# Shared rows copied one pair earlier in GpSimd's order, a small copy ahead of each early gather, and the first zeros made first

## The chip, the cores and the metric

The kernel runs on one core of a Trainium2 chip. The metric is the device time of one execution in microseconds (us), the median of the runs that are given. One execution is also recorded by the hardware profiler; its records give the span from the first to the last instruction and every engine's instructions in it.

## The reference, cut to what matters

```python
# attention: 8 batches, 8 heads, 576 positions, 64 wide; window 32, dilation 4
rel = pos[:, None] - pos[None, :]
mask_plain = (rel >= 0) & (rel < window)                                       # heads 0-3
mask_dil = (rel >= 0) & (rel < window * dilation) & (rel % dilation == 0)      # heads 4-7
scores = np.where(masks, q @ k.T / 8, -1e9)
attn = softmax(scores); x = attn @ v          # heads side by side: (8, 576, 512)
# mixture of 8 experts, one per token
logits = x @ w_gate; local_gate = sigmoid(x @ w_local)
for b, s:                                     # in order along s
    fresh_e = argmax(logits[b, s])
    e = fresh_e if s == 0 or local_gate[b, s] < 0.5 else prev_e
    prev_e = e
    out[b, s] = softmax(logits[b, s])[e] * (relu(x[b, s] @ w1[e]) @ w2[e])
```

Routing depends on the attention's result, and a token may inherit the expert of the token before it.

## The kernel before, in words

**Attention.** The host puts the positions of the dilated heads in order of their residue modulo 4, so that both kinds of head become a window of 32 neighbours. Work goes by pairs of heads: 8 batches times 4 pairs give `NPB = 32` pairs. A sequence is cut into 9 blocks of 64 queries; a block needs the 64 keys of its own block and the 32 before them, 96 in all. In SBUF the values of a pair lie in a tile `vt` of 96 partitions: rows 32 to 95 of block i are loaded from memory, and rows 0 to 31 are the last 32 rows of block i-1. These shared rows are not loaded a second time: `share(n)` (line 268) has GpSimd copy them from partitions 64 to 95 to partitions 0 to 31, for blocks 1 to 8. Block 0 has zeros there, set once. There are four such tiles (`AHEAD = 4`), used in turn.

**The loop** at line 1093 runs over n = 0 to 33. In turn n it issues the scores of pair n (TensorE, then ScalarE's exponentials with a VectorE clamp for the second half), `share(n)`, a slot for routing work (`gap`), `values(n - 1)` (line 367: products of the probabilities with `vt`, then VectorE's reciprocal into `rec` and a multiplication into `x`, once for slots 0 and 1, once for 2 to 4), on every second turn `turn` (line 390: transposes of x), another slot, the loads for pair n + 3, and the store of x. Then, if the list `rows` is not empty, one entry of it is run.

**The early gathers.** Routing of the first four batches ends in the midst of the loop (`early_tokens`, line 1082). It fills `rows` with eight indirect gathers (`rows_of`, line 842; DMA_INDIRECT of line 849) that fetch the tokens of the first two units of expert work out of the stored x. One is issued at the end of each turn from n = 26 on. The first four serve unit 0, whose `features(0)` (line 856, transposes of line 864) comes at the start of turn 33; the other four serve unit 1.

**What sets the order.** `manual_schedule` (line 216) keeps TensorE, VectorE, GpSimd and SyncE in the order in which the program text issues their instructions; each engine runs its own in that order and waits on semaphores. So GpSimd's order around the gathers is: share(26), gather 1, share(27), gather 2, share(28), gather 3, and so on to share(31), gather 6, gather 7, gather 8. Loads run on SyncE's queue; the gathers are DMAs of GpSimd's queue. PSUM tiles of the loop come from four banks (`banks`, tag "bank") used by values, turn and routing alike, and two double banks for the scores.

**After the loop** come 8 experts' worth of units of tokens (pairs of 128 tokens with seven products in place of eight, and smaller ones), with the weights streamed in.

**The start.** VectorE sets `ones` (line 203), `zero` (251), `warm` (281), then `before` (300); TensorE multiplies `warm` with itself three times (line 283), before the first scores.

The lines about which the change turns:

```python
    def share(n):
        vt = vts[n % AHEAD]
        nc.gpsimd.tensor_copy(vt[:WIN, :, 1:], vt[QB:, :, :NB - 1])
...
        if n < NPB:
            share(n)
        gap(SHARE)
        if 1 <= n <= NPB:
            values(n - 1)
...
        if rows:
            rows.pop(0)()
```

Of the kernel before, what the change touches and what calls it, by code (L numbers as in the profile page):

```python
# [10 lines left out]
F32 = mybir.dt.float32  # L11
# [11 lines left out]
P = 128  # L23
# [14 lines left out]
NPB = B * NP  # L38
UNITS = ((0, 5), (5, 9))
SLOTS = (NB + 1) // 2  # L40
# [141 lines left out]
@with_exitstack  # L182
def dilated_attn_locality_moe_kernel(
    ctx: ExitStack,
    tc: tile.TileContext,
    qk: bass.AP,
    v: bass.AP,
    wgl: bass.AP,
    w1: bass.AP,
    w2: bass.AP,  # L190
    con: bass.AP,
    adm: bass.AP,
    msk: bass.AP,
    qmk: bass.AP,
    out: bass.AP,
):
    nc = tc.nc
    keep = ctx.enter_context(tc.tile_pool(name="keep", bufs=1))
    cst = keep.tile([P, C_ALL], F32, name="cst")
    wg = keep.tile([P, DK, LW], F32, name="wg")  # L200
    ones = keep.tile([P, P], F32, name="ones")
    bad = keep.tile([1, 1], I32, name="bad")
    nc.vector.memset(ones, 1.0)

    args = (qk, v, wgl, w1, w2, con, adm, msk, qmk, out, cst, wg, ones)
    again = whole(tc, False, bad, *args)

    with tc.If(again > 0):  # L208
        whole(tc, True, bad, *args)


@with_exitstack
def whole(ctx, tc, exact, bad, qk, v, wgl, w1, w2, con, adm, msk, qmk, out, cst, wg, ones):
    nc = tc.nc
    name = "exact" if exact else "plain"
    ctx.enter_context(tc.manual_schedule(engines={ET.PE, ET.DVE, ET.Pool, ET.SP}))
# [2 lines left out]
    def pool(name, bufs, **kw):  # L219
        return ctx.enter_context(tc.tile_pool(name=name, bufs=bufs, **kw))  # L220
# [5 lines left out]
    once = pool("once", 1)  # L226
# [4 lines left out]
    def room(to, i, name, shape):  # L231
# [9 lines left out]
    ins, work, xp, xtp = (attention.enter_context(tc.tile_pool(name=name, bufs=bufs))  # L241
                     for name, bufs in (("ins", AHEAD), ("work", 2), ("xp", 3), ("xtp", 2)))
# [3 lines left out]
    def bank(shape, name):  # L246
        return banks.tile(shape, F32, name=name, tag="bank")

    rec = once.tile([P, NPB, SLOTS, 2], F32, name="rec")
    zero = work.tile([1, D // 2], F32, name="zero", bufs=1)  # L250
    nc.vector.memset(zero, 0.0)
    for to in xd:
# [11 lines left out]
    def load_values(n):  # L264
        vt = vts[n % AHEAD]
        nc.sync.dma_start(out=vt[WIN:].rearrange("p u i e -> p (u i e)"), in_=v[n])

    def share(n):
        vt = vts[n % AHEAD]
        nc.gpsimd.tensor_copy(vt[:WIN, :, 1:], vt[QB:, :, :NB - 1])  # L270

    def load(n):
        load_keys(n)
        load_values(n)

    if not exact:
        am = work.tile([P, adm.shape[1]], BF16, name="am", bufs=1)
        nc.sync.dma_start(out=am, in_=adm)
        mk = work.tile([KW, 2, S - UNITS[1][0] * QB], BF16, name="mk", bufs=1)
        warm = work.tile([P, 512], F32, name="warm", bufs=1)  # L280
        nc.vector.memset(warm, 0.0)
        for _ in range(WARM):
            nc.tensor.matmul(bank([P, 512], "cold"), lhsT=warm[:, :P], rhs=warm, start=True, stop=True)
    load_keys(0)
# [17 lines left out]
    def load_first(i, part):  # L302

        rows = FK // 4
        nc.sync.dma_start(out=raw1[i][:, part * rows:(part + 1) * rows].rearrange("p m k f -> p (m k f)"),
                          in_=w1[i, :, part * rows * D:(part + 1) * rows * D])
# [60 lines left out]
    def values(n):  # L367

        vt = loaded[n][2]
        if n % 2 == 0:  # L370
            xs[n // 2] = xp.tile([P, SLOTS, 2, 2, DH], F32, name="x")
        x = xs[n // 2]
        pr = prob.pop(n)
        for a, z in HALVES:
            pv = bank([P, z - a, 2, VW], "pv")
            for k in range(a, z):
                for u in range(2):
                    for h in range(2):
                        i = min(2 * k + h, NB - 1)
                        c, p = next((c, p) for c, p in reversed(pr) if c <= i)  # L380
                        nc.tensor.matmul(pv[h * QB:(h + 1) * QB, k - a, u], lhsT=p[:, u, (i - c) * QB:(i - c + 1) * QB],  # L381
                                         rhs=vt[:, u, i], start=True, stop=True, tile_position=(0, h * QB),
                                         skip_group_check=True)
            r = rec[:, n, a:z]
            nc.vector.reciprocal(r, pv[:, :, :, DH])
            nc.vector.tensor_tensor(x[:, a:z, n % 2], pv[:, :, :, :DH],
                                    r.unsqueeze(3).to_broadcast([P, z - a, 2, DH]), op=Alu.mult)
        del loaded[n]

    def turn(m):  # L390

        x = xs[m]
        b, g = divmod(m, 2)
        if m % (2 * GB) == 0:
            routes[b // GB] = dict(xt=xtp.tile([P, 2, CH, GS], F32, name="xt"))
        xt = routes[b // GB]["xt"]
        s = b % GB * S
        full = S // P * P
        for c in range(CH):
            tp = bank([P, S // P, P], "tp")  # L400
            for k in range(S // P):
                nc.tensor.transpose(tp[:, k], x[:, k, c].rearrange("p u d -> p (u d)"), ident)
            nc.scalar.copy(xt[:, g, c, s:s + full], tp.rearrange("p k t -> p (k t)"))
        tp = bank([P, CH, S - full], "tp")
        for c in range(CH):
            nc.tensor.transpose(tp[:, c], x[:S - full, S // P, c].rearrange("p u d -> p (u d)"),
                                ident[:S - full, :S - full])
        nc.scalar.copy(xt[:, g, :, s + full:s + S], tp)

    def store(m):  # L410

        x = xs.pop(m)
        b, g = divmod(m, 2)
        full = S // P * P
        to = xd[g][b * S:(b + 1) * S]
        nc.sync.dma_start(out=to[:full].rearrange("(k p) f -> p k f", p=P),
                          in_=x[:, :S // P].rearrange("p k g u d -> p k (g u d)"))
        nc.sync.dma_start(out=to[full:], in_=x[:S - full, S // P].rearrange("p g u d -> p (g u d)"))
# [362 lines left out]
    def gap(add=None):  # L781
        if add is not None:
            credit[0] = min(credit[0] + add, add)
        alone = False
        while waiting and not alone and (add is None or credit[0] >= 0):
            f, cost, _ = waiting.pop(0)
            credit[0] -= cost
            if f:
                f()
            alone = add is None or not waiting or waiting[0][2]  # L790
# [7 lines left out]
    def now(push):  # L798
        for f in push:
            f()  # L800
# [55 lines left out]
    def features(u):  # L856
        kind = units[u]["kind"]
        rows = rows_in(u)
        xe[u] = mw.tile([P, DK, 2 * P], F32, name="xe")
        for j in range(tiles_of(u)):  # L860
            x = xg.pop((u, j)).rearrange("p g f -> p (g f)")
            tp = bank([P, DK, P], "tp")
            for kk in range(DK):
                nc.tensor.transpose(tp[:, kk, :rows], x[:rows, kk * P:(kk + 1) * P], ident[:rows, :rows])
            nc.scalar.copy(xe[u][:, :, j * P:j * P + rows], tp[:, :, :rows])
        if kind == "pair":
            xc[u] = mw.tile([P, 4, DK // 2, P], F32, name="xc", bufs=1)
            return sums_right(xc[u], *(xe[u][:, 2 * k:2 * k + 2, j * P:(j + 1) * P]
                                       for k in range(2) for j in range(2)))
        return []  # L870
# [222 lines left out]
    for n in range(NPB + 2):  # L1093
        if n < NPB:
            (scores_exact if exact else scores)(n)
        if n < NPB:
            share(n)
        gap(SHARE)
        if 1 <= n <= NPB:
            values(n - 1)  # L1100
        if n == NPB + 1:
            assert len(rows) <= 4
            now(features(0))
        if n >= 3 and n % 2 == 1:
            turn((n - 3) // 2)
            if (n - 3) // 2 % (2 * GB) == 2 * GB - 1:
                route((n - 3) // 2 // (2 * GB), n == NPB + 1)
        gap(SHARE)
        if n + 3 < NPB:
            load(n + 3)  # L1110
        if n >= 3 and n % 2 == 1:
            store((n - 3) // 2)
        if n in (11, 14, 17, 20):
            load_first(0, (n - 11) // 3)
        if n == NPB + 1:
            weights(0, True)
            weights(1, False)
        if rows:
            rows.pop(0)()
    now(rows)  # L1120
    attention.close()
# [159 lines left out]
```

## Time and profile before

| | |
|---|---|
| runs | 667.06, 668.27, 689.95 us; median 668.27 |
| the profiled execution | 670.79 us, of which its span is 668.9 |
| granted TensorE clock | 0.997 |
| PE (TensorE) | busy 649.8 us |
| PEld (its weight loads) | busy 571.0 us |
| DVE (VectorE) | busy 373.1 us |
| ACT (ScalarE) | busy 188.7 us |
| POOL (GpSimd) | busy 185.3 us; the 32 copies of line 270 are 34.7 of it |

A row of the timeline has the start and the duration in us, the engine, the line, the operation, the tiles (out<-in), the shape and a count; in square brackets stand the idle time of the engine before it and what is taken to have ended it. Where several semaphores are waited for, the bracket names the one that came last by this record, which can be a mere coincidence. A row of the waits has who waited, for whom, the us in total, how many times, and the longest. The end of a matmul is modelled, since matmuls overlap; its start is recorded.

### The profile page before, as it was taken

The page shows a single profiled execution, that of the slowest core. Times are in us where ns is not written, and L with a number is a line of the kernel's source. Part 1 is how long each engine was busy: PE and PEld are TensorE (multiplying, and loading weights), DVE is VectorE, ACT ScalarE, POOL GpSimd, SP SyncE. Part 2 cuts the span into 40 slices and gives each one's busy share as a digit, 9 for nine tenths or more (in the row PEclk, how much of TensorE's full clock was granted, in tenths as well). Part 3 has the DMA queues.
Part 4 walks back from the last instruction along what each step waited for, and adds up shares of the span by engine and source line. Part 5 has one row for each costly group of instructions (what it writes and reads, how often), then busy time and mean ns, then how long its engine had stood idle before and what let it go on. Part 6 is the DMA issues. An engine that isn't in the chain of part 4 may idle for free. (4 is left out here: it accounts for less than half of the span.)

```text
span 668.9 us, 15284 instructions
## 1 busy us (share of the span) xinstructions
PE 649.8 (97%) x6466; PEld 571.0 (85%) x6466; DVE 373.1 (56%) x755; ACT 188.7 (28%) x348; POOL 185.3 (28%) x162
## 2 busy tenths in 40 slices
PE   8999999989999999999999999999999999999996
PEld 6989888877678999999599988997889988899893
DVE  3558578574496596373447381827373627446441
ACT  3544343432212332222223223222222232213210
POOL 3322212141024320221551252314044213041011
PEclk9999999999999999999999999999999999999998
DMA  8989889838205299474543456541054452354001
GB/s 322 306 299 318 288 264 321 250 117 318 119 33 189 64 416 368 176 274 174 198 163 130 161 187 223 238 159 50 3 189 176 184 206 99 133 212 146 1 33 49
DMA packets 29358, 126.38 MB, mean 189 GB/s; under 512 B 4222, under 2 KB 13790, under 8 KB 25313
## 3 DMA queue, kind: packets, MB, share of 16 engines
q1 hardware_dynamic: 22480, 106.10, 44.0%
q0 software_dynamic: 6800, 19.21, 8.3%
q8 instruction: 53, 0.87, 0.5%
q14 instruction: 25, 0.20, 0.1%
HBM read 142.07 MB, written 19.20 MB: 241 GB/s over the span
## 5 line engine op out<-in xcount | busy, mean ns | idle before, releaser
L973 POOL DMA_INDIRECT out_dram<-y,tok x36 | 55.0, 1528 | 297.3 <-DVE y L1042 124.3
L945 PE MATMUL hp<-xc,sum 128*128 128x128 f32 x720 | 85.7, 275 | 1.0 <-DVE sum L812 1.0
L945 PEld LDWEIGHTS hp<-xc,sum 128*128 128x128 f32 x720 | 82.9, 192 | 1.4 <-PE hp L945 1.1
L1027 PE MATMUL yp<-sum,hc 128*128 128x256 f32 x360 | 82.6, 379 | 0.0
L955 DVE TENSOR_TENSOR h<-hp,h 128x512 f32<-128x512 f32 x45 | 30.9, 689 | 90.5 <-PE hp L945 89.8
L1027 PEld LDWEIGHTS yp<-sum,hc 128*128 128x128 f32 x360 | 68.2, 190 | 9.5 <-ACT y L1035 0.2
L1042 DVE SCALAR_TENSOR_TENSOR y<-yp,gate,y 128x256 f32<-128x256 f32 x45 | 21.7, 482 | 75.0 <-issue 49.2
L270 POOL COPY vt<-vt 32x1040 f32<-32x1040 f32 x32 | 34.7, 1087 | 92.3 <-DMA vt<-in_v_dram 62.3
L945 PE MATMUL hp<-xe,raw 128*128 128x128 f32 x480 | 58.8, 276 | 0.0
L945 PEld LDWEIGHTS hp<-xe,raw 128*128 128x128 f32 x480 | 56.6, 192 | 1.8 <-issue 1.5
L1027 PE MATMUL yp<-raw,h 128*128 128x256 f32 x240 | 57.0, 380 | 0.0
L849 POOL DMA_INDIRECT xg<-xd,tok x40 | 45.7, 1142 | 38.6 <-PE hp L945 15.3
L329 PE MATMUL two<-kq 64*96 64x64 f32 x1152 | 54.7, 245 | 0.0
L329 PEld LDWEIGHTS two<-kq 64*96 64x96 f32 x1152 | 52.6, 162 | 0.0
L1027 PEld LDWEIGHTS yp<-raw,h 128*128 128x128 f32 x240 | 44.4, 190 | 5.5
L949 ACT COPY h<-hp 128x512 f32<-128x512 f32 x45 | 26.3, 585 | 79.0 <-PE hp L945 74.2
L381 PE MATMUL pv<-vt,pr 96*64 96x65 f32 x1280 | 45.9, 224 | 2.3 <-POOL vt L270 2.1
L956 ACT ACTIVATE h<-h 128x512 f32<-128x512 f32 x45 | 28.3, 630 | 67.2 <-DVE h L955 63.2
L334 DVE SCALAR_TENSOR_TENSOR pr<-two,mk 96x512 f32<-96x512 f32 x32 | 21.9, 684 | 44.7 <-ACT pr L336 28.6
L849 POOL DMA_INDIRECT xg<-xd,pos x40 | 43.0, 1075 | 12.1 <-issue 10.1
L381 PEld LDWEIGHTS pv<-vt,pr 96*64 96x64 f32 x1280 | 40.8, 137 | 5.3 <-POOL vt L270 2.6
L1035 ACT ACTIVATE y<-yp,gate 128x256 f32<-128x256 f32 x45 | 21.2, 473 | 55.7 <-PE yp L1027 49.9
(222 smaller groups left out, 1006.7 us busy)
## 6 DMA issues: line engine op xcount, KB each, us to landing
raw<-in_w_dram SPq DMA_DIRECT2D x48, 2048.0 KB
kq<-in_qk_dram SPq DMA_DIRECT2D x32, 592.0 KB
vt<-in_v_dram SPq DMA_DIRECT2D x32, 292.5 KB
xd<-x SPq DMA_DIRECT2D x16, 512.0 KB
raw<-in_w_dram SPq DMA_DIRECT2D x4, 512.0 KB
xd<-x SPq DMA_DIRECT2D x16, 64.0 KB
xg<-xd,tok POOLq DMA_INDIRECT x40
xg<-xd,pos POOLq DMA_INDIRECT x40
```

Source lines behind the costliest of these rows:

```text
L270: nc.gpsimd.tensor_copy(vt[:WIN, :, 1:], vt[QB:, :, :NB - 1])
L329: nc.tensor.matmul(sc[:KW, u, (i - a) * QB:(i - a + 1) * QB], lhsT=kt[h, i * QB:i * QB + KW], rhs=qt[h, i * QB:(i + 1) * QB], start=bool(a ...
L334: nc.vector.scalar_tensor_tensor(pr, sc[:KW, :, :w], -CEIL, mk[:, kind].unsqueeze(1).to_broadcast([KW, 2, w]), Alu.max, Alu.min)
L381: nc.tensor.matmul(pv[h * QB:(h + 1) * QB, k - a, u], lhsT=p[:, u, (i - c) * QB:(i - c + 1) * QB], rhs=vt[:, u, i], start=True, stop=True, ...
L849: nc.gpsimd.indirect_dma_start(out=x[:rows, g], out_offset=None, in_=xd[g] if units[u]["late"] else xd[g][:EARLY * GS], in_offset=bass.Ind ...
L945: nc.tensor.matmul(to[:, m], lhsT=a[:, m, kk], rhs=b[:, kk], start=first and m == 0 and kk == 0, stop=(kk == DK // 2 - 1), skip_group_chec ...
L949: nc.scalar.copy(at((0, 1, 3)[k]), of)
L955: nc.vector.tensor_tensor(at(k), of, at(k), op=Alu.add)
L956: nc.scalar.activation(at(k), at(k), Act.Relu)
L973: nc.gpsimd.indirect_dma_start(out=out, out_offset=bass.IndirectOffsetOnAxis(ap=of_unit(u, "tok", j), axis=0), in_=y, in_offset=None, boun ...
L1027: nc.tensor.matmul(to, lhsT=a[:, m], rhs=b[:, m], start=first and m == 0, stop=(m == FK // 2 - 1), skip_group_check=True)
L1042: nc.vector.scalar_tensor_tensor(at(k), of, of_unit(u, "gate", k // 2), at(k), Alu.mult, Alu.add)
```

## The change

1. `share` is issued for pair n + 1 in turn n, and for pairs 0 and 1 in turn 0.
2. Ahead of each early gather that turn n issues (n at most 32) stands a GpSimd copy of two numbers, from the last reciprocals of pair n - 1 into a tile `pace`.
3. The zeros `warm` are allocated in the pool that lives for the whole kernel, and are set ahead of everything else that VectorE does, also ahead of `ones`; before, they lay in a pool of the attention and were set after `ones` and `zero`. They take 2 KB of each partition, from then on to the end.

```diff
@@ dilated_attn_locality_moe_kernel
+    warm = keep.tile([P, 512], F32, name="warm")
+    nc.vector.memset(warm, 0.0)
     nc.vector.memset(ones, 1.0)
@@ whole
     rec = once.tile([P, NPB, SLOTS, 2], F32, name="rec")
+    pace = once.tile([1, 2], F32, name="pace")
...
+    def paced(n):
+        nc.gpsimd.tensor_copy(pace, rec[:1, n, SLOTS - 1])
+
     def share(n):
...
-        warm = work.tile([P, 512], F32, name="warm", bufs=1)
-        nc.vector.memset(warm, 0.0)
         for _ in range(WARM):
             nc.tensor.matmul(bank([P, 512], "cold"), lhsT=warm[:, :P], rhs=warm, start=True, stop=True)
@@ the loop
-        if n < NPB:
-            share(n)
+        for k in range(NPB)[n + 1 if n else 0:n + 2]:
+            share(k)
...
         if rows:
+            if n <= NPB:
+                paced(n - 1)
             rows.pop(0)()
```

More of the change, by code (lines that the diff above doesn't have):

```diff
@@ L202, in dilated_attn_locality_moe_kernel @@
     bad = keep.tile([1, 1], I32, name="bad")
+    warm = keep.tile([P, 512], F32, name="warm")
+    nc.vector.memset(warm, 0.0)
     nc.vector.memset(ones, 1.0)
-    args = (qk, v, wgl, w1, w2, con, adm, msk, qmk, out, cst, wg, ones)
+    args = (qk, v, wgl, w1, w2, con, adm, msk, qmk, out, cst, wg, ones, warm)
     again = whole(tc, False, bad, *args)
@@ L212, in whole @@
 @with_exitstack
-def whole(ctx, tc, exact, bad, qk, v, wgl, w1, w2, con, adm, msk, qmk, out, cst, wg, ones):
+def whole(ctx, tc, exact, bad, qk, v, wgl, w1, w2, con, adm, msk, qmk, out, cst, wg, ones, warm):
     nc = tc.nc
```

## The prediction

> **What bounds the kernel now.** I read the page first, then the waits of TensorE, then the timeline of TensorE and of GpSimd around the only place where those waits name GpSimd.
>
> ```profile
> PE 649.8 (97%) x6466; PEld 571.0 (85%) x6466; DVE 373.1 (56%) x755; ACT 188.7 (28%) x348; POOL 185.3 (28%) x162
> ...
> PE pv L381 <- POOL vt L270: 2.1, 4, 0.8
> PE cold L283 <- DVE before L300: 1.9, 1, 1.9
> ```
>
> TensorE sets the end: 668.9 - 649.8 = 19.1 us of idle time in the whole span. All that an edit outside TensorE's own work can win is in those 19.1 us. The two rows under it are the two that the diff touches: four waits of the value products (L381) for the shared rows, and the wait for `warm` before the first product. The timeline of TensorE shows the four:
>
> ```profile
> 135.06 0.33 PE L381 MATMUL pv<-vt,pr 96*64 96x65 f32 x2
> 136.00 1.38 PE L381 MATMUL pv<-vt,pr 96*64 96x65 f32 x38 [0.61 <-POOL vt L270]
> ...
> 140.76 0.33 PE L381 MATMUL pv<-vt,pr 96*64 96x65 f32 x2
> 141.32 1.38 PE L381 MATMUL pv<-vt,pr 96*64 96x65 f32 x38 [0.23 <-POOL vt L270]
> ...
> 144.67 0.33 PE L381 MATMUL pv<-vt,pr 96*64 96x65 f32 x2
> 145.82 1.38 PE L381 MATMUL pv<-vt,pr 96*64 96x65 f32 x38 [0.82 <-POOL vt L270]
> ...
> 149.23 0.33 PE L381 MATMUL pv<-vt,pr 96*64 96x65 f32 x2
> 149.95 1.38 PE L381 MATMUL pv<-vt,pr 96*64 96x65 f32 x38 [0.39 <-POOL vt L270]
> ```
>
> Block 0 needs no shared rows, so two matmuls start and the third waits. The bracket counts from a modelled end; a pair's 40 matmuls start 0.0325 us apart elsewhere, so the true delay is the third's start less the first's less 0.065: 0.88 + 0.50 + 1.08 + 0.66 = 3.11 us, not 2.1. These are values(28) to values(31). GpSimd there:
>
> ```profile
> 129.24 1.04 POOL L270 COPY vt<-vt 32x1040 f32<-32x1040 f32 x1 [3.17 <-issue]
> 130.55 1.01 POOL L849 DMA_INDIRECT xg<-xd,pos  x1 [0.27 <-POOL vt L270]
> 134.91 1.04 POOL L270 COPY vt<-vt 32x1040 f32<-32x1040 f32 x1 [3.35 <-PE two L329]
> 136.22 0.97 POOL L849 DMA_INDIRECT xg<-xd,tok  x1 [0.27 <-POOL vt L270]
> 140.23 1.04 POOL L270 COPY vt<-vt 32x1040 f32<-32x1040 f32 x1 [3.04 <-PE two L329]
> 141.54 1.00 POOL L849 DMA_INDIRECT xg<-xd,pos  x1 [0.27 <-POOL vt L270]
> 144.72 1.04 POOL L270 COPY vt<-vt 32x1040 f32<-32x1040 f32 x1 [2.19 <-PE two L329]
> 146.04 0.97 POOL L849 DMA_INDIRECT xg<-xd,tok  x1 [0.27 <-POOL vt L270]
> 148.86 1.04 POOL L270 COPY vt<-vt 32x1040 f32<-32x1040 f32 x1 [1.85 <-PE tp L406]
> ```
>
> Copies and gathers alternate, and a copy after a gather idles 1.85 to 3.35 us. Its own data had long landed (by the trace's landing signals 121.2, 126.4, 130.8 and 137.6 for pairs 28 to 31). The releaser named, TensorE, is a coincidence: the five gathers' landings are complete at 129.12, 134.79, 140.11, 144.61 and 148.74, and each copy starts 0.12 us after one. The copy waits until the gather before it has landed. So share(n) runs only when the gather of turn n - 1 has landed, in the midst of turn n + 1, just when values(n) wants it.
>
> At the start:
>
> ```profile
> 0.85 0.17 DVE L203 MEMSET ones<- 128x128 f32 x1 [0.85 <-PEq L1273]
> 1.01 0.27 DVE L251 MEMSET zero<- 1x256 f32 x1
> 1.33 0.48 DVE L281 MEMSET warm<- 128x512 f32 x1
> ```
>
> TensorE begins at 1.87, 0.06 after `warm` is set.
>
> [...]rows of 1.0 us, landings 2.7 to 4.2 us after the start. [...]4.1 to 4.2 while weights stream and 2.7 to 3.1 later, and I use these. [...]L585 (0.84 us alone) took 1.33 beside the copy that began at 108.31.
>
> **The change part by part.**
>
> *Order of the copies.* Up to turn 25 nothing stands between the copies in GpSimd's queue; each starts when its data land or its buffer is free, so issuing them a turn earlier moves nothing: 0 us. From turn 26 on each gather stands one copy later: share(27), gather 1, share(28), gather 2, and so on. share(27) no longer waits behind gather 1; it runs near 116.6. Gather 1 stays at 125.03: it waits for `tok` (VectorE, 124.17). Then share(28) starts at 129.24, where share(27) was. The old steps of that chain were 5.67, 5.32 and 4.49 us; each gets the small copy.
>
> *The small copy.* No row shows two elements. GpSimd's one-element memset took 0.10 us, its 130-element memset 0.26: I take 0.2 us, ends 0.05 and 0.5 with a semaphore. Its reciprocal is there early (122.6 for the first, 137.9 for pair 28's), so it waits for nothing that share has not waited for. Behind it queue only the gather and the next copy. Steps become 5.87, 5.52, 4.69: copies at 129.24, 135.1, 140.6, 145.3, the last done at 146.3. The gathers of unit 1 (5 to 8) are by now spaced by a landing each and end near 158 instead of 157.4, needed at 174.57: hidden. Gather 4 lands near 145.2; features(0) wants it after 148: hidden.
>
> *Where TensorE then stands.* Removing 3.11 us shows what is late next: VectorE, back to back from 132.0 to 138.5, and the banks it frees. Step by step, with durations from the timeline:
> values(28): third matmul 135.12, products issued by 136.36. The transposes of turn follow, but the small ones (L406) need the bank of pair 28's first half: reciprocal 137.09 (behind VectorE's scan), product to 137.69. L406 at 137.75 instead of 138.33, L488 and the next scores 0.72 earlier. Gain so far 0.72 of 0.88.
> values(29): VectorE's L499 is ready by 141.0, so L504 comes at 141.37 instead of 142.63: gain 1.26.
> values(30): L402 at 144.74 instead of 147.13: 2.39. VectorE's gate work (1.4 us after its clamp) lets pair 30's product end near 146.2, the bank for L542 at 146.33 against 148.72: still 2.39.
> values(31): starts 146.84, third matmul 146.9, and share(31) is done 146.3. features(0) at 148.17 instead of 151.26: 3.09.
> The last turn: its second half needs pair 31's product, which VectorE reaches after the routing chain that starts at 149.34 (147.2 now, moved by 2.14): 151.3 against 153.44. TensorE takes that half at 151.35 instead of 154.0: gain 2.65, and so the expert work starts at 154.08 instead of 156.73.
>
> *After that* TensorE waits 4.5 us in all to the end, for VectorE's sums and ScalarE, none for a DMA. SyncE's weight loads wait for TensorE (112 and 110 us in its list), so they move along. I carry 2.65 through.
>
> *`warm` first.* `ones` (0.17) and `zero` (0.27) with their gaps stood ahead: 1.33 - 0.85 = 0.48 us. TensorE starts at 1.39. Its next needs are covered: the first keys land at 5.14 against 6.26, later keys had 0.87 us or more to spare, share(0) ends 0.88 before it is wanted. Were the cover gone, 0.48 is lost. `zero` moves 0.5 us later, ahead of two tiny DMAs and a copy at 9.2. The 2 KB moved cost no instruction: 0.
>
> *Sum.* 0.48 + 2.65 = 3.13; I take off 0.2 for copies that now lie beside VectorE's two-input gate work (share(31), 145.3 to 146.3; up to 0.8 by the 0.49 seen at L585 and its length). 668.9 - 2.9 = 666.0 of span. That execution took 670.79, above the median of the runs, 668.27; taking the 2.9 from the median gives 665.4.
>
> **The rivals.**
> *VectorE takes the wait over.* For: it is back to back there and two of my steps already end on it[...]. Against: its chains shift too. Gain 3.13 - 2 x 0.8 = 1.5: 666.8.
> *Nothing arrives.* The copies are timely, but the freed time is given back before or in the expert work (the wait of 0.99 us for VectorE's sums at 220.95 grows, say). Against: no DMA is waited for. 668.3.
> *The chain ends on the other side.* GpSimd's step (about 5.4 us) is longer than a turn of TensorE without waits (three turns from 135.06 to 146.84, 3.9 us each); only the lead of one copy covers it. share(31) has 0.6 us left. From a mean step above 5.6 us it waits; above about 6.6 us the loss, three times the excess, eats the 3.1 us won. At 8 us, if the small copy also waited for something late, the kernel would be at 668.3 + 3 x 1.4 = 672.5. Against: the reciprocals are early. Over 2% (13.4 us) would take a step near 11 us.
>
> **How the numbers follow.** Forecast 0.60, VectorE 0.20, nothing 0.12, chain 0.08. A measurement of this kernel can tell about 2% from no change, and every case but the far end of the last lies within it. Low end: all 3.11 + 0.48 from the quickest run shown, 667.06 - 3.6 = 663.5. High end: a gain of 0.5 from the median, 667.8; this holds the forecast, VectorE's case and a part of the third, 8 in 10. The forecast's own range is 664.0 to 666.3. Faster by 2% would need 13.4 of the 19.1 idle us: 0.02. Slower 0.05, for the last case and what I do not see. Same 0.93.
>
> **What would show it.** The row of L381 waiting for L270 gone; the four pairs' matmuls start without a gap; copies and gathers alternating, each copy 0.12 after a landing, but one pair ahead; first product near 1.39; L919 first at about 153.6 (156.73 less 3.1). Wrong if share(31) ends after TensorE asks, if L406 or L402 wait longer for VectorE than here, or if L919's lead is lost later.

## The result and the profile after

After the change the median is 665.75 us (664.45 to 667.93, 18 runs); beside it the kernel before came to 672.02 us (666.91 to 689.95, 18 runs). The ratio is 0.9928, 95% interval 0.9902 to 0.9955. The forecast was 665.4 us and no difference of 2%.

The kernel before scatters more than the kernel after, and that has a part in the ratio: runs whose mean granted TensorE clock is below 0.995 are mostly 2 to 10 us longer, so I give means of the others as well, "at full clock" (a run with one stretch of 3.41 us at half clock, the shortest in the traces, still counts among these). At full clock the changed kernel has 665.9 us (all its 18 runs); the kernel before, in the first set of experiments, 668.5 us (51 of 75 runs). The difference is 2.6 us; the sum said 2.9. These two figures come from two sets of runs. The runs of the kernel before that stood beside the changed kernel have no clock on record; the nine of them below 671 us have a mean of 668.2. In two later sets, each with both kernels on one other chip, the difference is 4.0 and 3.5 us; what is added there is taken up with the small copies below.

The page of the profiled execution after (665.66 us, span 663.7), part 1, and the head of the waits of TensorE:

```profile
PE 648.9 (98%) x6466; PEld 570.0 (86%) x6466; DVE 373.4 (56%) x755; ACT 189.2 (28%) x348; POOL 190.7 (29%) x169
```

```profile
PE hp L949 <- DVE h L959: 1.7, 2, 0.9
PE cold L287 <- DVE warm L204: 1.5, 1, 1.5
PE tp L410 <- ACT xt L407: 1.0, 4, 0.2
PE tp L410 <- DVE rec L389: 0.9, 1, 0.9
PE pv L385 <- issue: 0.8, 1, 0.8
```

TensorE's idle time is 663.7 - 648.9 = 14.8 us, 4.3 less than before. The row of the values product (now L385) waiting for GpSimd's `vt` is gone. The timeline of TensorE, for the four pairs and the start of the expert work:

```profile
135.16 1.39 PE L385 MATMUL pv<-vt,pr 96*64 96x65 f32 x40
...
139.93 1.39 PE L385 MATMUL pv<-vt,pr 96*64 96x65 f32 x40
...
143.29 1.39 PE L385 MATMUL pv<-vt,pr 96*64 96x65 f32 x40
...
146.72 0.41 PE L546 MATMUL kp<-oh,cst 96*96 96x96 f32 x2 [0.44 <-DVE x L390]
...
147.23 1.39 PE L385 MATMUL pv<-vt,pr 96*64 96x65 f32 x40
148.54 1.09 PE L868 MATMUL tp<-cst,xg 128*128 128x128 f32 x8
...
154.19 3.07 PE L923 MATMUL hp<-xe,raw 128*128 128x256 f32 x13
```

Each pair's 40 products are one group again. The same stretch on GpSimd:

```profile
131.15 1.04 POOL L276 COPY vt<-vt 32x1040 f32<-32x1040 f32 x1 [4.39 <-PE two L333]
132.25 0.17 POOL L272 COPY pace<-rec 1x2 f32<-1x2 f32 x1
132.59 1.01 POOL L853 DMA_INDIRECT xg<-xd,pos  x1 [0.16 <-POOL pace L272]
135.59 1.04 POOL L276 COPY vt<-vt 32x1040 f32<-32x1040 f32 x1 [2.00 <-PE rp L482]
...
144.41 1.04 POOL L276 COPY vt<-vt 32x1040 f32<-32x1040 f32 x1 [2.03 <-PE pv L385]
```

By the landing signals the gathers were complete at 131.04, 135.48, 139.86 and 144.30; the copies of pairs 28 to 31 start 0.11 to 0.12 us after each. The alternation is the old one; only the pair is one ahead, and share(31) is done at 145.45, 1.8 us before TensorE wants it.

The span differs by 5.1 us between the two profiled executions. Matched instruction by instruction, 2.5 of it stands at L923's start, where the expert work begins (L919 before). The rest is not the change's: from there to the end the changed kernel takes 509.6 us, and the profile of the zeros alone, which keeps the old order of the copies, takes 509.5. The kernel before takes 512.1; about 1.4 of the excess is a pause at L987 near 416 us, named "issue", which the profiles of the first set lack and those of the two other chips have in part or whole (0.8 to 1.4 us).

### The profile page after: what moved, and what is told of

Its sections match the earlier page's. It is cut to its first block, busy times and chain, and to the rows that moved or that the text cites. A ratio compares the mean times of both kernels' runs of the same rounds, so it can differ in the third digit from the quotient of the medians.

```text
span 663.7 us, 15298 instructions
## 1 busy us (share of the span) xinstructions
PE 648.9 (98%) x6466; PEld 570.0 (86%) x6466; DVE 373.4 (56%) x755; ACT 189.2 (28%) x348; POOL 190.7 (29%) x169
## 5 line engine op out<-in xcount | busy, mean ns | idle before, releaser
L977 POOL DMA_INDIRECT out_dram<-y,tok x36 | 57.4, 1595 | 290.9 <-DVE y L1046 121.0
L385 PE MATMUL pv<-vt,pr 96*64 96x65 f32 x1280 | 44.6, 224 | 0.8 <-issue 0.8
L385 PEld LDWEIGHTS pv<-vt,pr 96*64 96x64 f32 x1280 | 40.0, 138 | 3.3 <-issue 1.5
```

The lines of the kernel that those rows point to most:

```text
L977: nc.gpsimd.indirect_dma_start(out=out, out_offset=bass.IndirectOffsetOnAxis(ap=of_unit(u, "tok", j), axis=0), in_=y, in_offset=None, boun ...
```

## The experiments

Three sets, each with its own runs of the kernel before on the same chip. The theory: the gain is the order of the copies, because a copy stands behind the landing of the gather ahead of it.

**First set: the parts** (the kernel before: 669.39 us; 668.5 at full clock).

The order alone:

```diff
-        if n < NPB:
-            share(n)
+        for k in range(NPB)[n + 1 if n else 0:n + 2]:
+            share(k)
```

> Only the copies are issued one pair earlier; no small copies, the zeros where they were. Order theory: all four waits of the value products for the shared rows are gone, L919 of the kernel before starts some 2.6 us earlier than in it, and the time is 2.5 to 5 us below the kernel before, as far as the whole change brings it (0.993). Pace theory (the held-back gathers are what helps, since a gather that runs ahead disturbs something): at most 1 us is won. Start theory: nothing is won.

Measured: 665.98 us, ratio 0.9954 [0.9933, 0.9975]; 665.9 at full clock, as the whole change. No wait for `vt` is left, and L919 starts 2.2 us earlier (154.49). The order carries the gain.

The small copies alone (`pace`, and `paced(n - 1)` ahead of each early gather):

> Only the small copies ahead of the gathers are added; copies of the shared rows in the old order. Order theory: the four waits stay, each longer by the 0.35 us that a small copy and its semaphore put between copy and gather (five gathers: up to 1.7 us), so the same as before or up to 1.7 us slower. Pace theory: 2.5 us faster or more.

Measured: 670.33 us, ratio 1.0017 [0.9990, 1.0045]; 669.7 at full clock, 1.2 more than before. Not faster, as the order theory had it. Whether each wait grew, its profile cannot tell: the clock was half from 138.12 us, and only the wait of pair 28 is left, 2.3 us long.

The zeros first, alone:

> Only the zeros are set first. TensorE's first product starts near 1.4 us instead of 1.87. If the earlier start carries through: 0.4 to 0.5 us faster, on average. If the moment at which the array reaches its full rate is set by something that does not move with the first product, [...]the time is the same within its interval. The four waits stay in either case.

Measured: 669.38 us, ratio 0.9993 [0.9973, 1.0014]; 668.65 at full clock. Nothing that can be told from no change. In its profile three of the four waits stand; pair 29's is missing.

Order and small copies:

> Copies earlier and small copies, the zeros where they were. Order theory: the time of the order alone within 0.5 us, since the small copies lie in GpSimd's slack: the copy of pair 31 ends at least 0.5 us before TensorE asks. Pace theory: better than the order alone by 1 us or more.

Measured: 666.74 us, ratio 0.9966 [0.9946, 0.9986]; 666.5 at full clock, 0.6 more than the order alone, which the scatter of these runs (some 1.2 us in each kernel, 19 runs each) does not tell from nothing. It is not better by 1 us, so the pace theory fails on this chip.

**Second set** (another chip; the kernel before: 674.03 us, 673.1 at full clock). Order and zeros, without small copies:

> The kernel before with the copies one pair earlier and the zeros made first, without the small copies. Theory (all of the gain is the order; the small copies cost some tenths and the zeros give nothing that lasts): the time of the order alone, about 665.9 us at full granted clock, ratio about 0.995 to 0.996, no row of L381 waiting for the shared rows. Rival 1 (the zeros give their 0.48 us): 665.4. Rival 2 (the small copies do some good in holding the gathers back, so that leaving them out costs): slower than the whole change, which runs beside it, by 0.5 us or more.

The whole change again:

> The changed kernel itself once more, on the chip of the parts. Theory: 665.7 us again, ratio 0.993 to 0.996, and within 0.5 us of order plus zeros. If the small copies cost what the first set hints at (they came out 0.65 us slower with the order than without, 1.2 us slower alone), it is 0.5 to 1 us slower than order plus zeros.

Measured: order and zeros 670.95 us, ratio 0.9963 [0.9944, 0.9983], at full clock 670.8; the whole change 669.35 us, ratio 0.9939 [0.9905, 0.9972], at full clock 669.1. Here the small copies were worth 1.8 us, against the theory and against the first set. The timeline of ScalarE shows a place where they differ. Order and zeros:

```profile
152.10 1.07 ACT L865 COPY xe<-tp 128x512 f32<-128x512 f32 x2 [4.87 <-remote]
```

The whole change:

```profile
151.39 1.07 ACT L869 COPY xe<-tp 128x512 f32<-128x512 f32 x2 [2.66 <-PE tp L868]
```

This is the first copy of features(0) out of PSUM. In the whole change it starts 0.31 us after the start of the fourth transpose that it waits for; in order and zeros 2.42 us after it. "Remote" means that the profile found no instruction to match the end of the wait. The trace's record of semaphores has it: the copy waits for TensorE's signal that the fourth transpose is done. That transpose starts at 149.68 and by the modelled ends is over at 149.95, but three signals of TensorE, of the value products and of the two halves of the transposes, are recorded together at 152.02, 152.07 and 152.13. After the change such signals come within 0.03 us of the modelled end. TensorE then waits for the copy:

```profile
152.74 1.79 PE L402 MATMUL tp<-cst,x 128*128 128x128 f32 x8 [2.35 <-ACT xe L865]
```

Two products of zeros in place of three, on order and zeros:

```diff
-WARM = 3
+WARM = 2
```

> Order plus zeros, with two products of zeros ahead of the first scores in place of three (these products only keep TensorE busy; nothing is computed with them). One product is two passes of 0.853 us, so the first scores may start 1.7 us earlier, at about 5.2 us, just when the keys have landed (5.14). Theory (the granted clock rises at a moment of its own, 5.0 to 7.5 us in the traces so far, whatever TensorE began with): the first scores run at half clock up to there, a net gain of 0.3 to 1.2 us against order plus zeros. Rival 1 (the start is covered by other work, ScalarE's exponentials or the keys): no difference.[...]

Measured: 672.10 us, ratio 0.9982 [0.9948, 1.0017]; 671.8 at full clock, 0.9 more than order and zeros. The first scores (L329) came at 5.53 us against 6.75, and the transposes of the first turns kept 0.5 us of that (18.20 against 18.71, up to 50.87 against 51.38). But at the next turn they were at 60.19 against 59.24, and near 90 us at 89.84 against 90.23. The kernel before has 89.89 there and the changed one 89.87. First scores between 5.53 and 7.14 us thus lead to turns within 0.4 us of one another at 90 us, and not in the order in which they started: in these four profiles the start does not set what comes later. The clock rose at 5.82 us against 6.20, not later, so a later rise does not explain the 0.9 us, which lie at the edge of the scatter; they stay open.

A memset ahead of four copies, on the kernel before:

```diff
     def share(n):
         vt = vts[n % AHEAD]
+        if n > 27:
+            nc.gpsimd.memset(junk, 0.0)
```

> The kernel before, with a GpSimd memset of 32 by 780 elements (an estimate of 1.1 us from 0.26 us for 130) ahead of each of the copies for pairs 28 to 31, into a tile that nobody reads. Theory (copies stand behind the landing of the gather ahead, and the chain copy, gather, landing sets TensorE's turns there): every step of the chain is 1.1 us longer, so the four waits of L381 grow from 3.1 us in all to about 7.3, and L923's counterpart comes 4 us later: 672 to 673 us in runs at full clock, ratio about 1.006. Rival (a copy is held by TensorE's work, as the profile's releasers say): the memset runs while GpSimd waits anyway, and the time stays within 0.5 us of before. On the granted clock: if the waits of the products at that place set off the stretches of half clock, they become more frequent than in the kernel before (24 of 75 runs with a mean clock below 0.995 so far): over half of the runs; if they come by themselves, about a third again.

Measured: 675.85 us, ratio 1.0014 [0.9992, 1.0036]; 674.7 at full clock, 1.7 more than before, not 4; 9 of 22 runs were below 0.995, as often as the kernel before in this set (26 of 57). The waits did not grow: in the profile the third products of the four pairs come 3.2 us late in all (2.9 in the kernel before, measured in the same way), not 7.3. The ratio is not clear of 1; ScalarE's first copy of features(0) is late here too, 2.81 us after the fourth transpose, and that may be what was lost. GpSimd's timeline says why the waits stayed:

```profile
133.19 1.01 POOL L852 DMA_INDIRECT xg<-xd,pos  x1 [0.27 <-DMA vt<-in_v_dram]
134.19 0.77 POOL L272 MEMSET junk<- 32x780 f32 x1
137.90 1.04 POOL L273 COPY vt<-vt 32x1040 f32<-32x1040 f32 x1 [2.94 <-PE rp L481]
```

The memset starts the moment the gather's row ends; the copy starts 0.11 us after that gather has landed (137.79). So GpSimd does not stand still until a landing; this one copy waits. The semaphore waits in the trace have it in so many words: every copy behind the first gather waits for its load, for TensorE and for the semaphore of the gather ahead (for this copy a wait instruction from 132.96 to 137.82); copies before that gather wait for GpSimd's own semaphore in its place. My theory was right in the place and wrong in the reason: it is a wait that the program contains, and work without it fits in front of it at no cost (0.77 us of it here, where I had estimated 1.1). Why the program has this wait, no run shows.

**Third set** (a third chip; the kernel before: 674.27 us, 672.1 at full clock).

> The changed kernel once more, as the neighbour for the next three on one chip: ratio to before 0.992 to 0.996, no wait of ScalarE's first copy of features(0).

Order and zeros, with gathers 5 to 8 taken out of the loop:

```diff
-        if rows:
+        if rows and n <= 29:
             rows.pop(0)()
```

> Order plus zeros, without small copies, and with only gathers 1 to 4 in the loop; gathers 5 to 8 (for the second unit) are issued after the loop, behind the transposes of features(0). Theory (in the second set, order plus zeros lost its 1.8 us against the whole change because the last gathers go out in a row just ahead of features(0), and ScalarE's first copy there starts 2 us late): no such late copy, and the time of the whole change or a few tenths less, on any chip. Rival (the late copy is a matter of the chip or of where the program lies, not of the gathers): as order plus zeros, be that with or without the late copy. Other side: the second unit's gathers land too late for its transposes near 172 us: slower by what is missing there, 1 us or more.

The shared rows of pairs 28 to 31 loaded by SyncE, on the kernel before (`share` returns at once for these):

```diff
         nc.sync.dma_start(out=vt[WIN:].rearrange("p u i e -> p (u i e)"), in_=v[n])
+        if n > 27:
+            up = v[n].rearrange("p (u i e) -> p u i e", u=2, e=VW)
+            nc.sync.dma_start(out=vt[:WIN, :, 1:], in_=up[QB - WIN:, :, :NB - 1])
```

> The kernel before, with the shared rows of pairs 28 to 31 loaded from memory by SyncE (133 KB for each pair) in place of GpSimd's copies; nothing then stands behind a gather's landing from pair 28 on, and seven gathers go out in a row from about 130 us. Theory (the four waits of L381 come only from the copies' wait for the landing ahead of them): no wait of L381 for shared rows, and the time of the order alone, 2.4 to 3 us less than before at full granted clock (ratio 0.995 to 0.997). Rival 1 (the loads of that time are the scarce thing: the DMA engines are 80 to 90% busy up to 130 us): L381 waits for the loads instead, no gain. Rival 2 (gathers in a row delay ScalarE or the loads): the gain is lost again by 1 to 2 us near features(0) or at 130 to 140 us.

Order and zeros again:

> Order plus zeros once more, beside the whole change. Theory (small copies do no good of themselves, cost 0.3 to 0.9 us): 0.3 to 0.9 us faster than the whole change, unless ScalarE's first copy of features(0) comes 2 us late as in the second set, in which case it is 1.5 to 2 us slower. Rival (the zeros or the missing small copies make the late copy in every run): the late copy again, on this chip too.

Measured: the whole change 668.55 us, ratio 0.9894 [0.9862, 0.9926], 668.6 at full clock; order and zeros 671.97, ratio 0.9959 [0.9931, 0.9986], 670.7 at full clock; late gathers 670.74, ratio 0.9956 [0.9927, 0.9985], 670.0 at full clock. The small copies are worth 2.1 us here, by six runs of the whole change. ScalarE's late copy is there again in order and zeros (2.31 us after the fourth transpose) and not in the whole change (0.31). The two profiled executions do not show the 2.1 us: that of order and zeros is 0.7 us shorter, because TensorE reached pair 28 at 134.90 against 137.84, and that of the whole change is the longest of its six runs.

The late gathers did not test what they were for. Nothing holds GpSimd back, so gathers 5 to 8 still went out in a row, at 152.47 to 156.32, around the transposes at 155.57; ScalarE's copy was late again (2.45 us).

Rows loaded by SyncE took 685.85 us (six runs, 685.28 to 688.27), ratio 1.0164 [1.0131, 1.0198]. The wait of the values products for the rows is gone, as the theory said, and the kernel is slower by far more than that. GpSimd's timeline, then TensorE's and VectorE's:

```profile
134.09 0.95 POOL L854 DMA_INDIRECT xg<-xd,tok  x1 [0.30 <-issue]
135.35 0.95 POOL L854 DMA_INDIRECT xg<-xd,pos  x1 [0.30 <-issue]
...
140.36 0.95 POOL L854 DMA_INDIRECT xg<-xd,pos  x1 [0.31 <-issue]
```

```profile
136.27 0.42 PE L334 MATMUL two<-kq 64*96 64x64 f32 x4 [0.36 <-issue]
...
138.48 0.38 PE L334 MATMUL two<-kq 64*96 64x64 f32 x4 [0.51 <-issue]
139.90 0.59 PE L334 MATMUL two<-kq 64*96 64x64 f32 x4 [1.04 <-issue]
...
142.96 0.89 PE L334 MATMUL two<-kq 64*96 64x64 f32 x6 [0.67 <-issue]
```

```profile
135.85 0.42 DVE L391 TENSOR_TENSOR x<-pv,rec 128x256 f32<-128x256 f32 x1
141.37 0.20 DVE L390 RECIPROCAL rec<-pv 128x6 f32<-128x6 f32 x1 [5.10 <-remote]
```

Seven gathers go out in a row, some 1.25 us apart, from 132.78 to 141.31. While they do, TensorE stops again and again in the midst of one pair's 36 products, which wait for nothing that the profile shows ("issue": 4.4 us in 8 waits). VectorE, and SyncE's next load, wait for TensorE's signal that pair 27's products are done. The last of these products starts at 134.36; the signal is recorded at 141.35, just after the last gather's row ends, and the two go on at 141.37 and 141.40. The last of TensorE's stops ends at 142.96, 0.36 us after the only transfer of instructions that the profile has between 135.2 us and that time: 16 KB of its queue kind "instruction", from 141.63 to 142.60. The added loads do not stand in the way meanwhile: no packet of SyncE's queue runs between 136.90 and 142.71.

Then TensorE's clock is half, from 139.68 to 170.40; all six runs have a mean clock of 0.974 to 0.977. 30.7 us at half clock do 15.4 us of work; the kernel lost 13.8 against its neighbours at full clock (685.9 - 672.1), so by this estimate it would have been about 1.6 us ahead without the fall.

Where this leaves the small copies: they keep the last gathers from going out in a row (147.56, 151.62, 153.43 after the change, against 146.99, 148.24, 149.49 with the order alone); the small copy ahead of the gather at 151.62 waited 2.43 us for pair 31's reciprocal. None of the five profiles of kernels with small copies shows ScalarE's late copy (0.31 us in four, 0.46 in the one that ran at half clock there). Of the kernels without them, five of the six profiled in the second and third set show it: it starts 2.3 to 2.8 us after the fourth transpose. The sixth (0.46) is the one with loaded rows, whose gathers were out 26 us earlier. The two of the first set (0.31) and the kernel before (0.77) do not show it. In all five profiles with the late copy, TensorE's signals come late and together, as in order and zeros; in four of them the first of the three comes 0.9 to 1.1 us after the row of the last gather ends (with the longer memset, 0.4).

So in these profiles gathers in a row go together with late signals of TensorE (or late work behind them, since ends are modelled), and in the kernel with loaded rows with stops of TensorE, the last of which ends 0.36 us after a transfer of instructions. What holds up TensorE's work or its signals, and whether it is the same in both, no run shows. ScalarE's own instructions are not shown to be late. Why the first chip was spared, with the same row of gathers, stays open; there the small copies cost 1.2 us without the order, and with it 0.6, which is within the scatter.

## Why the prediction was right, point by point

*The bound and the four waits.* Right: TensorE sets the end, the waits are gone, the order alone gives the gain. At full clock 2.6 us were gained of 2.9, and the order alone gives 2.6 too; on the other two chips the small copies add to it. The spacing was misread: in an undisturbed pair the third product starts 0.11 us after the first, not 0.065, because the first four do not start evenly. Against such a pair the third products were 2.9 us late in all and the last products 3.3 us; the 3.11 lies between.

*The reading of the copies' idle time.* Right that the named releaser is a coincidence and that the landing releases the copy. In order alone the profile names the gather itself for one of them. That it is an explicit wait of the copy I had not seen, though the trace has it.

*GpSimd's chain.* Forecast 129.24, 135.1, 140.6, 145.3; measured 131.15, 135.59, 139.98, 144.41. Mis-sized twice, with opposite signs. The first gather started at 125.72 (125.03 taken) and landed 5.3 us later (4.1 taken), so the first copy came 1.9 us late. The three steps after it took 4.4 us each where I had 5.87, 5.52 and 4.69 from the old chain, because those gathers landed 2.8 to 2.9 us after their start. (In the old chain the third took 3.9 us, which the ranges of the prediction leave out.) The end came out 0.9 us early. This is one execution: in two more profiles of the same kernel the steps are 5.0, 4.5, 4.5 and 5.5, 5.4, 4.5 us, nearer to the forecast, and there too share(31) ends 1.9 us before it is wanted. What makes a gather land sooner stays open.

*The small copy.* 0.2 taken, 0.17 to 0.18 measured. That it has no other effect was wrong: without the order 1.2 us were lost on one chip, and with it 1.8 to 2.1 won on two. The second I did not see: I had called the gathers of unit 1 hidden and asked only when they land, not what they do to others when they go out in a row.

*TensorE's steps.* Before the four pairs the trace after is 0.11 us late (134.99 against 134.88 at the product ahead of values(28)). Taking that out, the gains are 0.92 at the small transposes (0.72 forecast), 1.49 at L508 (1.26), 2.63 at L406 (2.39), 2.11 at L546 (2.39), 2.83 at features(0) (3.09) and 2.65 at L923 (2.65). VectorE is late next where I had put it: L546 waits 0.44 us for pair 30's product, the last turn's second half 0.34 and 0.19. So the first rival was there and took no more than the working gave it. That the last figure is met to 0.01 us is partly luck: the steps before it are off by up to 0.3 us to either side. What the 0.2 taken off for copies beside VectorE's gate work was worth cannot be told. (The row of L585 that the prediction calls alone lies beside the copy that began at 110.46, which took 1.28 us in place of 1.04, so its 0.84 is no measure of L585 undisturbed.)

*After that.* "4.5 us of waiting, none for a DMA": the gain of L923 is kept to the end (509.6 us of expert work after it, 509.5 with the zeros alone), so the second rival fell. But 1.5 of the 4.5 us were no wait for VectorE or ScalarE: they are named "issue", at L987, and are gone in the profile after. The third rival did not come: the steps were 4.4 us, and 5.5 at most in the other two profiles, under the 5.6 that it needs.

*`warm` first: this step failed.* TensorE's first product came at 1.47 (before 1.87; 1.39 forecast), but its scores at 7.14 against 6.87 (6.08 and 7.18 in two more profiles of the same kernel), and the gain of 0.48 us was not there. Alone, the zeros gave a ratio of 0.9993. Two things stand against it. The clock rose at 7.08 us after the change, at 4.85 and 7.42 in those two profiles, all with the first product at 1.47, and at 6.03 before, with the first product at 1.87; the six passes of zeros took 4.50 us with the earliest rise and 5.49 with the two latest. And a lead at the start was gone by 90 us: first scores at 5.53 us (two products of zeros) and at 7.14 led to 89.84 and 89.87 there.

*The median.* Taking 2.9 from the median of three runs met 665.75 within 0.4 us. That is luck in part: the median of these three, 668.27, lay near the mean at full clock (668.5), while the kernel before has medians of 669 to 674 in larger sets. A part of the ratio is therefore the clock, which the sum did not contain. The span was forecast at 666.0 and is 663.7; the 2.3 us that it is short are about what lay behind L919 in the one profile of the kernel before. And the 0.48 us of the zeros, which did not come, stood in the sum against the 0.2 taken off.

## What to carry to other kernels

When an instruction waits just behind a transfer on the same queue, look in the list of semaphore waits before blaming the engine or the releaser that the profile names; then put the instruction ahead of that transfer. Before unchaining a row of indirect gathers, ask what paces them: here the kernel in which seven of them went out in a row lost 13.8 us, with TensorE at half clock for 30.7, while the four waits that this removed came to about 3. A saved fraction of a microsecond at the start counts only if a later turn still has it: here 0.5 us at 51 us was no lead at 60.

## What was not expected of the hardware

**Pauses of TensorE of 1.68 to 2.74 us were followed by a longer stretch at half clock.** The granted clock in the traces falls to half for stretches of 3.41 to 30.72 us. (Those at the very start and the very end are left out.) In the fourteen profiled executions, each of the nine single pauses of TensorE of 1.68 us or more (up to 2.74) after the start was followed by such a stretch, within 1.7 us of its end or already in it; none of the five pauses of 1.28 to 1.56 us was (the ends of matmuls are modelled, so these lengths are good to some tenths). The eight profiles with the nine pauses have mean clocks of 0.980 to 0.997; the other five, that with loaded rows apart, 0.997 to 0.999. What sets off a stretch, and what its length, no run shows. The longest stretch, 30.72 us, is that of the kernel with loaded rows, where none of the stops is longer than 1.04 us but they come in a row. The clearest is the kernel with small copies alone, whose first gather of the chain started at 126.29 (125.03 in the kernel before), with the copy behind it at 131.91 (129.24). Its timeline of TensorE:

```profile
136.26 0.33 PE L385 MATMUL pv<-vt,pr 96*64 96x65 f32 x2
138.62 2.43 PE L385 MATMUL pv<-vt,pr 96*64 96x65 f32 x38 [2.03 <-POOL vt L274]
```

and the clock row of its page:

```profile
PEclk9999999957999999999999999999999999999999
```

The wait of 2.03 us was one of the four that the change removes; the clock was half from 138.12 to 162.01, and the 38 products took 2.43 us instead of 1.38. By an estimate (half of the 23.89 us) the stretch cost some 12 us on top of the pause; this execution took 678.71 us, and the runs of its kernel at full clock 669.7.

It also bears on the result: of the runs of the kernel before in my three sets, 66 of 166 were below a mean clock of 0.995; of the changed kernel's, 2 of 36. On the first chip it was 24 of 75 before, 9 of 22 with the small copies alone and 3 of 22 with the order alone. That the removed waits and the gathers' spacing bring this about is what these counts and the traces suggest. The longer memset, which was to make it more frequent, is no test of it, since the waits did not grow.
